# Decode step of two layers: the second attention's scores one unit further ahead on TensorE

## The chip, the cores and the metric

The kernel runs on one core of a Trainium2 chip. The metric is the device time in microseconds (us) of one execution. Engines: TensorE (PE; PEld is its weight load), VectorE (DVE), ScalarE (ACT), GpSimd (POOL) and SyncE (SP), which issues nearly all DMAs.

## The reference, cut to what matters

One token for each of 4 batches passes through attention, a gated layer, the same attention and the same gated layer, each on a layer norm and added to x. The weights and the caches are the same for both layers.

```python
W = 2048                                   # the last 2048 of 8192 cached positions
q = (layernorm(x) @ wq)                    # 32 heads of 128, 8 KV heads, 4 query heads to each
s = einsum("bhqd,bhkd->bhqk", q, k) * 128 ** -0.5
o = einsum("bhqk,bhkd->bhqd", softmax(s), v)
x = x + o @ wo
h = sigmoid(layernorm(x) @ w_gate) * (layernorm(x) @ w_up)   # 512 -> 1792
x = x + h @ w_down                          # then both once more
```

## The kernel before, in words

**Memory.** One SBUF arena holds all that is loaded: 16 buffers of 1 MB for K (two for each KV head) and 9 more that rotate. K is loaded once and stays, transposed in place in the first attention, until the second has used it. V is loaded for each attention; of the last head, one half stays in its buffer and the other is stashed in PSUM and brought back. The output projection wo stays too. `loads` is the list of what is still to come, in a fixed order. Whenever a buffer is released (`done`, or `pool.release` in `score`, line 1078), `fill` takes the next load and writes its DMA into SP's program; it waits there for the last reader of the buffer. For the second attention the list is: V of seven units (14 loads, 1 MB each), w_gate (2), w_up (2) and w_down (3 pieces) of the second gated layer.

**Order.** The kernel is a list of operations. `_Plan.op` works out each one's dependencies from the tokens it reads and writes and from PSUM banks: an operation on a bank waits for all that another engine last did in that bank. From the second attention on `P.chain` is set (line 1296), so TensorE runs its operations exactly in the order in which they are written down, by hand, in `attn_second`. SP too follows that order. VectorE, ScalarE and GpSimd are ordered by `_schedule`, a list scheduler that works with modelled times. Every operation waits for its dependencies in its engine's queue, in order.

**A unit** of the second attention is one KV head with its 16 rows of queries; eight units, 2.0 to 2.7, run from head 7 down to head 0. Its steps:

- `q_unit` (called `qx`): four matmuls spread the unit's queries in bank CB (L721), ScalarE copies them to one of two halves of `qbd` (L726).
- `score`: the mask (L751, 4 matmuls) and the scores (L762, 16) into a bank; it then frees the unit's two K buffers and fills them with the next loads. Unit 2.0 has the bank OBS[0], 2.1 the bank WB, later ones SB[0] and SB[1] in turn.
- `soft`: on VectorE the maximum (L773), its exchange between halves (L777), the mask (L781) and the column's maximum (L785); on ScalarE the exponential (L788) into `prow`, of which there is one only, with the row sums.
- `turn` (`turn_p`): TensorE permutes P (L801), ScalarE copies it back into `prow` (L803), VectorE transposes it into one of two halves of `ebuf` (L808).
- `sum_up`: for units 2.0 to 2.6 `sums`: GpSimd (L904), a matmul (L909), a reciprocal on VectorE (L911), GpSimd (L914). For 2.7 `sums_old`: four small GpSimd steps (L817 to L821), three matmuls (L827), a reciprocal (L834).
- `pv_wide`: 16 matmuls of P times V (L931), transposed (L939), reduced (L944) and moved (L946) on VectorE, added and scaled on GpSimd (L948, L951). For 2.7 it is `pv_unit`, in two halves (L850), with `wo_compact` of unit 2.6 (L1000) between them.
- `back` (`o_back`): two matmuls transpose the result (L965), in bank WB, for unit 2.6 in CB; ScalarE copies it (L971).
- `wo`: the output projection (L984), summed over the units; `wo_back` brings that sum back by a ScalarE copy (L1010) and four matmuls (L1016).

TensorE's order in the loop over u before the change: P times V of u, turn of u+1, back of u-1, scores of u+2, sums of u+1, qx of u+3, projection of u-1. In the last round (u = 6) back and projection of 2.5 come first, then P times V of 2.6, turn of 2.7, `wo_back` and the sums of 2.7.

After the attention come `attn_add` (L1137, L1141), the layer norm and the second `glu`: gate and up matmuls (L1179), transposes (L1188), the product hT (L1206), w_down in three pieces (L1220), copies (L1231) and the output's DMA.

Of the kernel before, what the change touches and what calls it, by code (L numbers as in the profile page):

```python
# [278 lines left out]
def build(nc, A_x, A_k, A_v, A_wq, A_wo, B_wg, B_wu, B_wd, out, cfg=None):  # L279
# [8 lines left out]
    NW = cfg.get("NW", 7)  # L288
# [33 lines left out]
    with es:  # L322
# [559 lines left out]
        def wide_buffers(s, op):  # L882
            f = tile_ap(s).bitcast(F32)
            n = 0
            for name, size in (("tv", 512), ("o32", 32), ("osh", 32), ("rm", 64), ("rv", 8), ("pr", 8)):
                for k2 in range(2):
                    rest[name, k2] = f[:, n:n + size]
                    if name == "tv":
                        rest["dg", k2] = f[:, n:n + 544]
                    n += size  # L890
            for k2 in range(2):
                rest["A", k2] = f[:, n:n + 128].bitcast(BF16)
                n += 128
            rest["op"] = op
            rest["mb"] = f[:, n:n + 64]
            P.op("gpsimd", "mb", 200.0,
                 lambda g: g.tensor_copy(rest["mb"].rearrange("p (b x) -> p b x", b=2),
                                         maskb.unsqueeze(2).broadcast_to([128, 2, 32])),
                 r=[("maskb",)], w=[("mb",)], after=(op,))

        def sums(tag, k2):
            pr, rv, rm = (rest[n, k2] for n in ("pr", "rv", "rm"))
            P.op("gpsimd", "pr" + tag, 200.0,
                 lambda g: g.tensor_scalar(pr, sel_r[:, :], psm[:, k2:k2 + 1], None, ALU.mult),  # L904
                 r=[("psm", k2), ("sel_r",)], w=[("pr", k2)], after=(rest["op"],))
            sbank, c0 = (CB, 256) if tag == "2.0" else (WB, k2 * 8)
            out_ = ps[0:64, sbank, c0:c0 + 8]
            P.op("tensor", "sb" + tag, tm["pe_f32"],
                 lambda pe: pe.matmul(out_, rest["mb"], pr, start=True, stop=True),  # L909
                 r=[("pr", k2), ("mb",)], w=[("psb", k2)], banks=(sbank,))  # L910
            P.op("vector", "ri" + tag, c_dve(8) + 60.0, lambda v: v.reciprocal(rv[0:64, :], out_),  # L911
                 r=[("psb", k2)], w=[("rinv", k2)], banks=(sbank,))
            P.op("gpsimd", "rm" + tag, 250.0,
                 lambda v: v.tensor_tensor(rm[0:64, :].rearrange("p (x e) -> p x e", e=8),  # L914
                                           rv[0:64, :].unsqueeze(2).broadcast_to([64, 8, 8]),
                                           maske[0:64, :].unsqueeze(1).broadcast_to([64, 8, 8]), ALU.mult),
                 r=[("rinv", k2), ("maske",)], w=[("rm", k2)])

        def pv_wide(tag, h, k2, tiles):
            ob = OBS[k2]  # L920
            ew = ebuf[:, k2 * 256:(k2 + 1) * 256].bitcast(BF16).rearrange("p (g n x t) -> p g n t x", g=4, n=2, t=2)
            ss = dict((bp, need(name)) for bp, name in tiles)

            def e_pv(pe):
                last = None
                for n in range(4):
                    mq, t = n // 2, n % 2
                    for g in range(4):
                        jh, bp = g // 2, g % 2
                        src = tile_ap(ss[bp])[:, (jh * 16 + 8 * mq) * 128:(jh * 16 + 8 * mq + 8) * 128]  # L930
                        last = pe.matmul(ps[32 * g:32 * g + 32, ob, :], ew[:, g, mq, t],  # L931
                                         src.rearrange("p (m t d) -> p t m d", t=2, d=128)[:, t], start=(n == 0), stop=(n == 3))
                return last
            P.op("tensor", "PV" + tag, 16 * tm["pe_row"], e_pv,
                 r=tok(ss[0]) + tok(ss[1]) + [("e", k2)], w=[("pso", k2, 0), ("pso", k2, 1)], banks=(ob,))
            for bp, name in tiles:
                done(name)
            tv, o32, osh, rm, av = (rest[n, k2] for n in ("tv", "o32", "osh", "rm", "A"))
            P.op("vector", "tv" + tag, c_dve(512), lambda v: v.transpose(tv, ps[:, ob, :]),  # L939
                 r=[("pso", k2, 0), ("pso", k2, 1)], w=[("tv", k2)], banks=(ob,), after=(rest["op"],))  # L940

            def e_rd(v):
                dg = rest["dg", k2].rearrange("p (m y) -> p m y", m=4)[:, :, 0:128].rearrange("p m (q z) -> p q z m", z=32)[:, :, 0:8, :]
                return v.tensor_reduce(o32.rearrange("p (q x) -> p q x", x=8), dg, AXX, ALU.add)  # L944
            P.op("vector", "rd" + tag, c_dve(128), e_rd, r=[("tv", k2)], w=[("o32", k2)])
            P.op("vector", "sh" + tag, tm["dve_small"], lambda v: v.tensor_copy(osh[0:64, :], o32[64:128, :]),  # L946
                 r=[("o32", k2)], w=[("osh", k2)])
            P.op("gpsimd", "ad" + tag, 250.0, lambda v: v.tensor_tensor(o32[0:64, :], o32[0:64, :], osh[0:64, :], ALU.add),  # L948
                 r=[("o32", k2), ("osh", k2)], w=[("o32", k2)])
            P.op("gpsimd", "av" + tag, 500.0,  # L950
                 lambda v: v.tensor_tensor(  # L951
                     av[0:64, :].rearrange("p (x q e) -> p x q e", x=8, q=4),
                     o32[0:64, :].rearrange("p (q x) -> p x q", x=8).unsqueeze(3).broadcast_to([64, 8, 4, 8]),
                     rm[0:64, :].rearrange("p (x e) -> p x e", e=8).unsqueeze(2).broadcast_to([64, 8, 4, 8]), ALU.mult),
                 r=[("o32", k2), ("rm", k2)], w=[("av", k2)])
            late["tr", tag] = lambda: o_back(tag, k2, av)
# [101 lines left out]
        def attn_second():  # L1058
            hs = list(range(HKV))[::-1]

            def tag(u):
                return "2.%d" % u

            def turn(u):
                turn_p(2, tag(u), u % 2, PBS[0], u < NW)

            def qx(u):
                if u < HKV:
                    q_unit(tag(u), hs[u], u % 2)

            def score(u):
                if u >= HKV:
                    return
                softmax_unit(tag(u), hs[u], True, False)
                if u == 0:
                    soft(0)
                for bp in range(2):
                    pool.release(4 * hs[u] + 2 * bp)
                fill()

            def soft(u):
                if u < HKV:
                    late.pop(tag(u))()

            def sum_up(u):
                if u < NW:
                    sums(tag(u), u % 2)
                elif u < HKV:
                    sums_old(tag(u), u % 2)

            qx(0)
            score(0)
            qx(1)
            q_mms(1, 0, OBS[1], (0, 1))
            score(1)
            turn(0)
            qx(2)
            s = need(wq_part(1, NC - 1, 0)[0])
            left[wq_part(1, NC - 1, 0)[0]] += 1
            q_mms(1, 0, OBS[1], (2, 3))  # L1100
            wide_buffers(s, P.ops[-1])
            sum_up(0)
            q_turn(1, 0, OBS[1], rest["tv", 1], [("tv", 1)], [o for o in P.ops if o.name == "pt2.0"])
            soft(1)
            op = {}

            def wo(u):
                wo_wide(tag(u), hs[u], op[u], u % 2, u == 0, u == NW - 2)

            def back(u):  # L1110
                op[u] = late.pop(("tr", tag(u)))()

            for u in range(NW):
                if u == NW - 1:
                    back(u - 1)
                    wo(u - 1)
                pv_wide(tag(u), hs[u], u % 2, v_tiles[(2, hs[u])])
                turn(u + 1)
                if 0 < u < NW - 1:
                    back(u - 1)  # L1120
                score(u + 2)
                soft(u + 2)
                if u == NW - 1:
                    wo_back()
                sum_up(u + 1)
                qx(u + 3)
                if 0 < u < NW - 1:
                    wo(u - 1)
            u = NW

            def between():
                wo_compact(tag(u - 1), hs[u - 1], late.pop(("tr", tag(u - 1)))(), (u - 1) % 2)
            wo_unit(tag(u), hs[u], pv_unit(tag(u), hs[u], u % 2, v_tiles[(2, hs[u])], between), u % 2, False, True)
# [236 lines left out]
```

## Time and profile before

| what | us |
|---|---|
| median of 6 runs | 184.06 (183.44 to 184.86) |
| the profiled execution's own time | 183.44 |
| its span in the profile | 181.7 |
| TensorE busy, share of the span | 99.5, 55% |
| VectorE busy | 101.7, 56% |
| ScalarE busy | 32.9, 18% |
| GpSimd busy | 21.5, 12% |
| DMA: 72.09 MB | mean 397 GB/s |

The profile is of one execution; its times count from the span's start. The span is less than the execution's own time by 1.7 us, which lie around it. A line of the timeline has start, duration, engine, source line, operation, output and inputs with shape, and how often; in brackets stands the idle time of the engine before it and what ended it. The chain of waits is followed back from the last instruction, at each step to what released it. TensorE's mean granted clock is 0.965 of the full one.

### The profile page before, as it was taken

How to read it: one execution, taken by the hardware profiler on the slowest of the kernel's cores; microseconds unless marked ns; L12 is line 12 of the kernel's file. 1: busy time of each engine (PE TensorE's matmuls, PEld its weight loads, DVE VectorE, ACT ScalarE, POOL GpSimd, SP SyncE). 2: the span in 40 equal slices, each digit the busy share in tenths (PEclk: the TensorE clock that was granted, in tenths of full speed). 3: DMA queues.
4: the chain of work that ended last, by engine and by line, in shares of the span. 5: the costliest groups of instructions: out<-in, count | busy, mean ns of one | idle time of the engine just before them, and what ended most of it. 6: DMA issues, size and time to landing. Idle time of an engine off the chain costs nothing.

```text
span 181.7 us, 3839 instructions
## 1 busy us (share of the span) xinstructions
PE 99.5 (55%) x1627; PEld 53.5 (29%) x1639; DVE 101.7 (56%) x253; ACT 32.9 (18%) x87; POOL 21.5 (12%) x86
## 2 busy tenths in 40 slices
PE   1435325672725619245266566455948876756672
PEld 1002111342411505214136441331213333325531
DVE  6208997758484393653944633122776777744351
ACT  2002032121120301203003001001223444332011
POOL 7000010110010100101001000000012333333000
PEclk9999999999999999999999999999996999999567
DMA  5999999999999999999999999999999999999960
GB/s 190 418 429 433 418 418 415 415 429 415 414 423 418 426 418 416 417 422 426 408 420 418 409 404 409 405 385 390 412 427 420 422 418 424 418 405 407 411 273 20
DMA packets 12305, 72.09 MB, mean 397 GB/s; under 512 B 1144, under 2 KB 1152, under 8 KB 5632
## 3 DMA queue, kind: packets, MB, share of 16 engines
q1 hardware_dynamic: 12280, 71.84, 96.5%
q8 instruction: 13, 0.21, 0.5%
q14 instruction: 4, 0.03, 0.0%
q10 hardware_dynamic: 8, 0.00, 0.0%
HBM read 71.83 MB, written 0.00 MB: 395 GB/s over the span
## 4 chain that ended last, share of the span: by engine, by line
DMA 42%; DVE 24%; PE 22%; SPq 4%; ACT 3%; issue 3%; POOL 0%; DVEq 0%; ACTq 0%
DMA arena<-in_A_v_cache_dram 23%; PE ps L762 9%; DMA arena<-in_B_w_down_dram 9%; DVE arena L733 9%; DMA arena<-in_A_wq_dram 5%; DMA arena<-in_B_w_up_dram 5%; DVE nmax L773 4%; SPq L398 4%; PE ps L751 3%; ACT prow L788 3%; DVE nmax L777 2%; PE ps L850 2%; DVE mxt L781 2%; PE ps L1030 1%; PE ps L674 1%
## 5 line engine op out<-in xcount | busy, mean ns | idle before, releaser
L733 DVE STREAM_TRANSPOSE arena<-arena 128x1024 f32<-128x1024 f32 x32 | 37.0, 1202 | 0.0
L762 PE MATMUL ps<-arena,qbd 128*32 128x512 bf16 x256 | 26.1, 544 | 0.0
L850 PE MATMUL ps<-ebuf,arena 128*128 128x8 bf16 x576 | 17.7, 168 | 9.4 <-DMA arena<-in_A_v_cache_dram 5.3
L773 DVE TENSOR_REDUCE nmax<-ps 128x1 f32<-128x512 f32 x16 | 11.1, 691 | 20.8 <-PE ps L762 20.8
L751 PE MATMUL ps<-msk_m,msk_s 128*32 128x512 bf16 x64 | 8.6, 527 | 22.0 <-DVE arena L733 21.8
L850 PEld LDWEIGHTS ps<-ebuf,arena 128*128 128x128 bf16 x576 | 16.7, 104 | 11.5 <-DMA arena<-in_A_v_cache_dram 6.4
L788 ACT ACTIVATE prow<-ps,nmax 128x512 bf16<-128x512 f32 x16 | 11.0, 687 | 37.9 <-DVE nmax L785 35.5
L726 ACT CAST qbd<-ps 128x256 bf16<-128x256 f32 x16 | 6.0, 373 | 47.9 <-PE ps L762 34.8
L674 PE MATMUL ps<-arena,xn 128*4 128x512 bf16 x64 | 7.9, 577 | 7.6 <-DMA arena<-in_A_wq_dram 6.5
L817 POOL CAST s<-psm 128x1 bf16<-128x1 f32 x9 | 1.7, 188 | 84.6 <-ACT prow L788 84.2
L762 PEld LDWEIGHTS ps<-arena,qbd 128*32 128x32 bf16 x256 | 8.5, 121 | 10.5 <-issue 7.8
L803 ACT CAST prow<-ps 128x512 bf16<-128x512 f32 x16 | 9.4, 586 | 10.9 <-PE ps L801 2.1
L808 DVE STREAM_TRANSPOSE ebuf<-prow 128x256 f32<-128x256 f32 x16 | 7.0, 438 | 5.0 <-ACT prow L803 4.9
L687 DVE STREAM_TRANSPOSE ebuf<-ps 128x512 f32<-128x512 f32 x3 | 2.1, 717 | 11.9 <-PE ps L674 11.8
L751 PEld LDWEIGHTS ps<-msk_m,msk_s 128*32 128x32 bf16 x64 | 1.8, 101 | 23.4 <-DVE arena L733 19.0
L655 ACT ACTIVATE lnv<-ps 128x4 f32<-128x4 f32 x4 | 0.7, 174 | 41.7 <-PE ps L651 41.7
L931 PE MATMUL ps<-arena,ebuf 128*32 128x512 bf16 x112 | 8.1, 415 | 0.0
L721 PE MATMUL ps<-qh,eyew 32*128 32x64 bf16 x64 | 5.7, 220 | 4.3 <-ACT qbd L726 2.4
L1179 PE MATMUL ps<-arena,xn 128*4 128x448 bf16 x64 | 6.6, 553 | 2.4 <-DMA arena<-in_B_w_up_dram 1.6
L858 DVE TENSOR_TENSOR onb<-ps,rinv 128x16 bf16<-128x16 f32 x9 | 1.7, 185 | 10.6 <-PE ps L850 10.6
L801 PEld LDWEIGHTS ps<-prow,perm 128*128 128x128 bf16 x16 | 1.6, 100 | 18.3 <-ACT prow L788 17.9
L939 DVE STREAM_TRANSPOSE arena<-ps 128x512 f32<-128x512 f32 x7 | 5.0, 711 | 3.0 <-PE ps L931 3.0
(105 smaller groups left out, 125.9 us busy)
## 6 DMA issues: line engine op xcount, KB each, us to landing
arena<-in_A_v_cache_dram SPq DMA_DIRECT2D x30, 1024.0 KB, 18.5
arena<-in_A_k_cache_dram SPq DMA_DIRECT2D x16, 1024.0 KB, 25.1
arena<-in_A_wq_dram SPq DMA_DIRECT2D x8, 1024.0 KB, 9.0
arena<-in_A_wo_dram SPq DMA_DIRECT2D x4, 1024.0 KB, 25.0
arena<-in_B_w_gate_dram SPq DMA_DIRECT2D x4, 896.0 KB, 16.2
arena<-in_B_w_up_dram SPq DMA_DIRECT2D x4, 896.0 KB, 15.9
arena<-in_B_w_down_dram SPq DMA_DIRECT2D x2, 1024.0 KB, 12.9
arena<-in_B_w_down_dram SPq DMA_DIRECT2D x1, 768.0 KB, 7.4
```

The source lines that it names most:

```text
L398: o = P.op("sync", name, 0.0, lambda e, dst=dst, src=src: e.dma_start(dst, src), r=r, w=w, dma_bytes=nbytes, dma_rate=tm[rate])
L674: last = pe.matmul(ps[32 * hh:32 * hh + NB, qb, :], xn[:, c * NB:(c + 1) * NB], tile_ap(s)[:, o + hh * 512:o + (hh + 1) * 512], start=(c = ...
L733: P.op("vector", "T%d_%d" % (h, t), c_dve(1024), lambda v, v32=v32: v.transpose(v32, v32), r=[("slot", 4 * h + t)], w=[("slot", 4 * h + t)])
L751: last = pe.matmul(ps[32 * gi:32 * gi + 32, bank, :], msk_s[:, :], msk_m[:, :].unsqueeze(1).broadcast_to([128, 256, 2]), start=True, stop= ...
L762: last = pe.matmul(ps[32 * gi:32 * gi + 32, bank, :], qbd[:, q0:q0 + 32], kt[:, cp // 2, cp % 2, jh * NJ:(jh + 1) * NJ, :], start=False, s ...
L773: lambda v: v.tensor_reduce(nmax[:, k2:k2 + 1], ps[:, bank, :], AXX, ALU.max),
L788: lambda a: a.activation(prow[:, :].rearrange("p (m x t) -> p m x t", x=32, t=2), ps[:, bank, :].rearrange("p (m t x) -> p m x t", x=32, t ...
L803: P.op("scalar", "pc" + tag, c_act(512), lambda a: a.copy(prow[:, :], ps[:, pb, :]), r=[("ppb", pb)], w=[("prow",)], banks=(pb,))
L808: P.op("vector", "pt" + tag, c_dve(256), lambda v: v.transpose(et, prow[:, :].bitcast(F32)), r=[("prow",)], w=[("e", k2)])
L850: last = pe.matmul(ps[:, ob, bp * 8:bp * 8 + 8], src[:, j * 128:(j + 1) * 128], ev[:, j % 2, j % 16 // 2, x0:x0 + 8], start=(j == 0), stop ...
L931: last = pe.matmul(ps[32 * g:32 * g + 32, ob, :], ew[:, g, mq, t], src.rearrange("p (m t d) -> p t m d", t=2, d=128)[:, t], start=(n == 0) ...
L1179: last = pe.matmul(ps[32 * g:32 * g + NB, OBS[n], 0:NF], xn[:, c * NB:(c + 1) * NB], tile_ap(s)[:, o:o + NF], start=(c == 0), stop=(c == N ...
```

## The change

Three things change, and no computation is added or left out.

1. The scores of unit 2.2 are put ahead of the sums of 2.0, and the qx of 2.3 ahead of the loop; in the loop the scores are those of u+3 in place of u+2, and qx that of u+4 in place of u+3. `soft` keeps its place: that of u+2 now comes a round after its scores. The K buffers are freed, and the loads that take them are issued, with the scores.
2. In the last round, the turn of 2.7 and its sums come ahead of P times V of 2.6.
3. The sums of unit 2.6 are in bank CB, no longer in WB.

```diff
-            sbank, c0 = (CB, 256) if tag == "2.0" else (WB, k2 * 8)
+            sbank, c0 = (CB, 256) if tag in ("2.0", "2.%d" % (NW - 1)) else (WB, k2 * 8)
...
             wide_buffers(s, P.ops[-1])
+            score(2)
             sum_up(0)
             q_turn(1, 0, OBS[1], rest["tv", 1], [("tv", 1)], [o for o in P.ops if o.name == "pt2.0"])
             soft(1)
+            qx(3)
...
             for u in range(NW):
                 if u == NW - 1:
                     back(u - 1)
+                    turn(u + 1)
                     wo(u - 1)
+                    sum_up(u + 1)
                 pv_wide(tag(u), hs[u], u % 2, v_tiles[(2, hs[u])])
-                turn(u + 1)
+                if u < NW - 1:
+                    turn(u + 1)
                 if 0 < u < NW - 1:
                     back(u - 1)
-                score(u + 2)
+                score(u + 3)
                 soft(u + 2)
                 if u == NW - 1:
                     wo_back()
-                sum_up(u + 1)
-                qx(u + 3)
+                else:
+                    sum_up(u + 1)
+                qx(u + 4)
                 if 0 < u < NW - 1:
                     wo(u - 1)
```

## The prediction

> **What bounds the kernel now.** I read the page's slices first, then the chain that ended last, the SP queue, the tail instruction by instruction, and the DMA rate by stretch. The slices:
>
> ```profile
> DMA  5999999999999999999999999999999999999960
> GB/s 190 418 429 433 418 418 415 415 429 415 414 423 418 426 418 416 417 422 426 408 420 418 409 404 409 405 385 390 412 427 420 422 418 424 418 405 407 411 273 20
> ```
>
> The 16 DMA engines are full from 4.5 us to about 174 us. 71.8 MB have to come in, and no slice of the second attention (about 126 to 169 us) has a hole. The chain shows the attention first, one unit every 4.29 us, and then leaves it for a DMA:
>
> ```profile
> 151.93 0.70 DVE nmax L773
> ...
> 153.55 0.79 ACT prow L788 x2
> ...
> 154.38 0.39 PE ps L801
> ...
> 155.23 0.94 PE ps L762 x14
> 156.19 0.70 DVE nmax L773
> ...
> 162.52 0.38 SPq L398
> ...
> 162.94 15.76 DMA arena<-in_B_w_down_dram
> ...
> 178.74 0.31 PE ps L1220 x8
> ```
>
> Within a unit, scores (L762), maximum (L773), exponential (L788), permutation (L801) and the next scores form one ring: 156.19 - 151.93 = 4.26. But the last 16 us are one transfer, the last piece of w_down, which waits in line behind the others. SP shows that the line is long:
>
> ```profile
> 144.96 3.40 SPq L398 DMA_DIRECT2D arena<-in_B_w_gate_dram  x2
> 148.40 8.84 SPq L398 DMA_DIRECT2D arena<-in_B_w_up_dram  x2
> 157.29 6.69 SPq L398 DMA_DIRECT2D arena<-in_B_w_down_dram  x3
> ```
>
> An issue takes 0.37 us when there is room (w_gate's first). These take about 4.4 us each: SP is held back by a full queue, not by a buffer. From the trace's semaphore records (16 increments per transfer, one for each engine's share) I take when transfers are complete: V of unit 1 at 134.0, of unit 5 at 155.1, of unit 6 at 160.0, of unit 7 at 162.5 and 165.0, second half of w_up at 174.4, the w_down pieces at 176.8, 178.1 and 178.7. The first increments come every 2.48 us per MB without a gap. The last increment trails the first by 1.6 us at 126 us and by 3.7 us at the end: a few engines are late.
>
> The tail:
>
> ```profile
> 176.87 0.22 DVE L1206 TENSOR_TENSOR hT<-ebuf,qbd 128x56 bf16<-128x56 f32 x1
> 177.20 0.46 PEld L1220 LDWEIGHTS ps<-arena,hT 128*4 128x4 bf16 x32 [1.31 <-DMA arena<-in_B_w_down_dram]
> 177.23 0.62 PE L1220 MATMUL ps<-arena,hT 128*4 128x128 bf16 x32 [1.04 <-DVE hT L1206]
> 178.12 0.21 PEld L1220 LDWEIGHTS ps<-arena,hT 128*4 128x4 bf16 x16 [0.46 <-DMA arena<-in_B_w_down_dram]
> 178.12 0.40 PE L1220 MATMUL ps<-arena,hT 128*4 128x128 bf16 x16 [0.27 <-DMA arena<-in_B_w_down_dram]
> 178.74 0.28 PE L1220 MATMUL ps<-arena,hT 128*4 128x128 bf16 x8 [0.23 <-DMA arena<-in_B_w_down_dram]
> ```
>
> Two paths meet here. Compute: hT at 177.09, after which the three groups would take 0.62 + 0.40 + 0.28 = 1.30, from 177.23 to 178.53. DMA: the third piece at 178.70, the last group done at 179.02. So compute has 179.02 - 178.53 = **0.5 us of slack**, and the DMA sets the end. After it come fixed copies and the output, up to 181.7. The last view is the DMA by stretch:
>
> ```profile
> 174.00:175.00 1.00, 1.00 (x14) 0.72 (x14) 0.65 (x1) 0.37 (x3) 0.00 (x0) 0.50 0.84 336
> 175.00:176.00 1.00, 1.00 (x24) 0.37 (x12) 0.61 (x3) 0.35 (x3) 0.00 (x0) 0.68 0.51 207
> 176.00:177.00 1.00, 0.18 (x8) 0.00 (x0) 0.96 (x3) 0.00 (x0) 0.00 (x0) 1.00 0.26 107
> 177.00:178.00 1.00, 0.62 (x32) 0.46 (x32) 0.08 (x1) 0.00 (x0) 0.00 (x0) 1.00 0.23 88
> ```
>
> The last three numbers are granted clock, DMA share and GB/s. From 176 on, a quarter of the engines is still working: the stragglers finish alone.
>
> **What the Trainium skill says.** "DMA: Bandwidth & Descriptors", section "Why a DMA increments its semaphore by 16 and not by 1": the engines of one transfer finish independently, and only the full count means that all landed. The trace agrees (3.7 us between first and last increment). "Runtime: NRT & Kernel Launch", section "Instruction fetch mechanics": an engine's instructions come in 16 KiB blocks over a DMA queue of its own. The page's third part has q8 with 13 packets and 0.21 MB, so 16 KB each, and the straggling grows by 1.0 us where one of them ran at 136.8. The change adds no instruction, so I expect the same 13. "TensorE: Matmul & The Clock Gate", section "What's actually happening": the clock is halved after idle windows. Here it was 0.5 from 138.1 to 141.5 and from 168.8 to 175.6; at half clock the 16 P x V matmuls took 1.90 us against 1.04.
>
> **The change, part by part.**
>
> *Scores one unit further ahead.* S(2) is moved ahead of the first unit's P x V, and inside the loop S(u+3) takes the place of S(u+2), as qx(u+4) does of qx(u+3). No work is added: per unit still 0.40 mask, 1.1 scores, 0.28 qx on TensorE. What goes is the ring. The maximum of u+2 then finds its scores done a unit earlier. Left over is the ring of the one buffer prow: exponential 0.88, permutation 0.39, copy 0.59, transpose 0.45, with steps of about 0.06 between, 2.5 us. VectorE has 0.69 + 0.33 + 0.25 + 0.21 + 0.16 + 0.72 + 0.38 + 0.18 + 0.45 = 3.37 a unit, with gaps of 0.03 about 3.6; TensorE about 3.4 (154.38 to 157.76). So a unit can fall from 4.29 to about 3.6, 0.7 x 6 = 4 us in all, **but V arrives at one unit per 5 us**. The second half of unit 7's P x V, now at 168.25, can't start before 165.0. The attention gains at most **3.2 us**.
>
> *What the loads do.* S(u) frees two K buffers, so each V and weight load can be issued about one unit (4.29 us) earlier; order and sizes stay. SP's queue is full from 145 on and no engine runs dry before that: earlier issues only wait longer in line. Worth **0**. Its cover is the full queue; were it gone, an issue would be earlier, never later.
>
> *Start-up.* S(2), 0.40 + 1.47 at the first units' rate, now stands ahead of unit 0's sums, and qx(3), 0.28, ahead of its P x V. qx(3) writes the bank in which unit 0's sums lie, so it waits for their reciprocal on VectorE, which may stand behind unit 1's maximum (done at 136.2). P x V(0), now at 133.5, may start at up to 136.6, 3.1 late. Its transpose was taken up at 136.09 anyway, and the permutation of unit 1, at 137.03, waits for its exponential. After a P x V up to 137.65 that is **0 to 0.6 us** late; I take 0.6.
>
> *Sums of the seventh unit in bank CB.* The transposition of unit 5 (162.31) waited for the reciprocal of unit 6 (162.01) because both use bank WB. That wait goes: part of the gain above, at most the 1.3 us that TensorE idled there.
>
> *Last P turned ahead of its V.* Permutation (0.39) and sums of unit 7 (0.22) move ahead of P x V(6). The sums wait for four GpSimd steps of 0.19 with gaps, 163.02 to 164.00: a new wait of 1.0 us after the last exponential, with P x V(6), the output projection and unit 6's whole back end queued behind it. On GpSimd these four stand ahead of unit 6's steps, as they do now. Its gain is that transpose and P of unit 7 are ready at once. Taken together with the order now, from the last exponential to the last half P x V: before 168.25 - 162.96 = 5.3; after 1.35 + 1.04 + 2.3 (VectorE and GpSimd to unit 6's transposition, by 164.34 to 166.80 now) + 1.0 = 5.7, **0 to 0.4 us worse**, covered because the last exponential itself no longer waits for S(7) and can be up to 2 us earlier (unit 6's transpose was done at 160.14, the exponential started at 162.18).
>
> *Sum.* Attention ends 3.2 us earlier at best, and 0.6 + 0.4 = 1.0 later if nothing of the ring is gained; likeliest 1.5 to 3 earlier. Then w_up is late next: hT at the earliest 174.4 + 0.74 (half of the 16 matmuls of 1.48) + 0.59 + 0.22 + 0.1 = 176.0, against 177.09. And then the DMA: last piece 178.70, unchanged. **Change of the span: 0.**
>
> The sum is against the profiled execution, 183.44 us (span 181.7, 1.7 around it), the fastest of six. The median is 0.62 higher. Whether that is DMA or a run in which compute was late by more than its 0.5 us the page can't say; the second kind would be cured. I take a quarter of it: 184.06 - 0.16 = **183.9**.
>
> **The rivals.**
>
> *A: the DMA still sets the end* (forecast): 183.4 to 184.4. For it: full queue, gapless increments, 0.5 us of slack. Against it: nothing in the page, only that the six runs spread by 1.4 us.
>
> *B: faster, the stragglers are fewer.* If the instruction blocks or other traffic fall on other engines, the remaining work of 0.84 + 0.51 + 0.26 + 0.23 + 0.08 = 1.9 us after 174 ends at 175.9; compute then ends at 176.0 + 0.14 + 1.30 = 177.4 instead of 179.02: 1.6 less, 182.5. It needs compute to be earlier too, which this change gives. Against it: nothing in the change moves bytes between engines.
>
> *C: slower, P x V waits for work that isn't its own.* P x V(0) starts 3.1 us late behind qx(3), and VectorE's planned order puts each maximum behind the transpose before it, so that the ring stays at 0.88 + 0.39 + 0.59 + 0.45 + 1.5 + steps = 4.2 and the loss is carried to the end. It decides from 0.5 (slack) + 0.9 = 1.4 us carried; at 2.0 carried, with the tail's 0.4 added, 184.06 + 1.9 = 186.0; at 1.5, 185.1. For it: the planner's order is by modelled times. Against it: VectorE has 0.9 us to spare per unit, and V's pace is slower than the ring.
>
> *D: the order doesn't come out as stated*, since engines other than TensorE are ordered by the planner: same time as A, 184.06.
>
> **How the numbers follow.** A 0.63, D 0.07, B 0.18, C 0.12. About 0.5% (0.9 us) is what a measurement of this kernel can tell from no change. A and D lie within it but for 0.02 on the faster side: faster 0.2, same 0.68, slower 0.12. The range has to leave out at most 0.2: from the upper part of B (182.9) to the lower part of C (185.1).
>
> **What would show it.** Right: last w_down piece at 178.7 within 0.5; the chain ends in the same transfer; units of about 5 us with P x V waiting for V's DMA; PE idle before w_up at 174. Ring broken: no wait of the permutation for the exponential of 0.9 us. Wrong: a last landing before 178 (B), or hT later than 177.6 with the chain running through attention (C).

## The result, and the profile after

The changed kernel takes 183.6 us (median of 36 runs, 182.77 to 184.07), the kernel before 184.13 (73 runs, 183.07 to 186.12). The ratio is 0.9965 with a 95% interval of 0.9952 to 0.9978: 0.64 us less, 0.4 to 0.9. The lowest times differ by 0.3 us, the highest by 2.05: what the change takes away is mostly the upper part of the old spread.

The profiled execution of the changed kernel took 183.27 us, its span 181.5. The slices of its page are as full as before:

```profile
DMA  5999999999999999999999999999999999999960
GB/s 199 415 428 431 421 418 418 412 428 417 415 422 419 422 419 415 417 424 426 408 422 415 409 404 413 406 385 382 421 417 424 424 419 421 419 410 410 408 280 20
```

In the second attention, TensorE's timeline shows P x V of units 2.0, 2.1, 2.2 and 2.3 (start, duration):

```profile
134.69 1.05 PE L931 MATMUL ps<-arena,ebuf 128*32 128x512 bf16 x16
138.45 1.05 PE L931 MATMUL ps<-arena,ebuf 128*32 128x512 bf16 x16 [0.18 <-DVE nmax L785]
...
141.85 1.05 PE L931 MATMUL ps<-arena,ebuf 128*32 128x512 bf16 x16
145.20 1.04 PE L931 MATMUL ps<-arena,ebuf 128*32 128x512 bf16 x16
```

Unit 2.2 takes 3.35 us (145.20 - 141.85) where a unit took 4.29. From unit 2.4 on V is late instead. P x V of 2.5 and 2.6 and the two halves of 2.7 wait for it, and a unit takes 5.36 us (160.28 - 154.92):

```profile
154.92 1.05 PE L931 MATMUL ps<-arena,ebuf 128*32 128x512 bf16 x16 [1.67 <-DMA arena<-in_A_v_cache_dram]
...
160.28 1.05 PE L931 MATMUL ps<-arena,ebuf 128*32 128x512 bf16 x16 [0.29 <-DMA arena<-in_A_v_cache_dram]
...
162.69 0.96 PE L850 MATMUL ps<-ebuf,arena 128*128 128x8 bf16 x32 [0.38 <-DMA arena<-in_A_v_cache_dram]
...
165.20 1.01 PE L850 MATMUL ps<-ebuf,arena 128*128 128x8 bf16 x32 [0.31 <-DMA arena<-in_A_v_cache_dram]
```

The last half P x V starts at 165.20 (before: 168.25). Then the tail:

```profile
174.18 0.92 PE L1185 MATMUL ps<-arena,xn 128*4 128x448 bf16 x8 [1.34 <-DMA arena<-in_B_w_up_dram]
...
175.84 0.22 DVE L1212 TENSOR_TENSOR hT<-ebuf,qbd 128x56 bf16<-128x56 f32 x1
...
176.63 1.02 PE L1226 MATMUL ps<-arena,hT 128*4 128x128 bf16 x32 [1.11 <-DMA arena<-in_B_w_down_dram]
...
177.85 1.02 PE L1226 MATMUL ps<-arena,hT 128*4 128x128 bf16 x24 [0.20 <-DMA arena<-in_B_w_down_dram]
```

hT is ready at 176.06, 1.03 us earlier than before. It can't be earlier, because the last matmuls ahead of it wait for the second half of w_up, and behind it TensorE waits for w_down. The chain of waits no longer runs through the units' ring:

```profile
160.28 1.07 PE ps L931 x16
161.35 0.65 SPq L398
...
162.05 15.77 DMA arena<-in_B_w_down_dram
177.81 0.04 issue
177.85 0.60 PE ps L1226 x16
```

By the semaphore records the pieces of w_down are complete at 176.6, 177.8 and 178.45 (before 176.8, 178.1 and 178.70). Three us earlier at the attention's end are 1 us at hT and 0.2 us at the end of this execution. So the question is where the 0.64 us over all the runs come from.

### The profile page after: what moved, and what is told of

It reads as the page before. It is cut to its first block, busy times and chain, and to the rows that moved or that the text cites. A ratio compares the mean times of both kernels' runs of the same rounds, so it can differ in the third digit from the quotient of the medians.

```text
span 181.5 us, 3837 instructions
## 1 busy us (share of the span) xinstructions
PE 100.3 (55%) x1627; PEld 53.7 (30%) x1639; DVE 101.2 (56%) x253; ACT 32.5 (18%) x87; POOL 21.3 (12%) x86
## 4 chain that ended last, share of the span: by engine, by line
DMA 54%; DVE 20%; PE 15%; SPq 4%; issue 3%; ACT 3%; DVEq 0%; ACTq 0%
DMA arena<-in_A_v_cache_dram 35%; DMA arena<-in_B_w_down_dram 9%; DVE arena L733 9%; PE ps L762 6%; DMA arena<-in_A_wq_dram 5%; DMA arena<-in_B_w_up_dram 5%; SPq L398 4%; DVE nmax L773 3%; PE ps L751 2%; ACT prow L788 2%; PE ps L850 2%; PE ps L1030 1%; DVE ps L507 1%; DVE arena L517 1%; DVE nmax L777 1%
## 5 line engine op out<-in xcount | busy, mean ns | idle before, releaser
L762 PE MATMUL ps<-arena,qbd 128*32 128x512 bf16 x256 | 25.4, 531 | 0.0
L931 PE MATMUL ps<-arena,ebuf 128*32 128x512 bf16 x112 | 7.3, 381 | 3.4 <-DMA arena<-in_A_v_cache_dram 2.0
L1030 PE MATMUL ps<-onp,arena 128*128 128x16 bf16 x144 | 5.3, 175 | 2.4 <-DVE onp L873 2.4
```

Source lines behind the costliest of these rows:

```text
L762: last = pe.matmul(ps[32 * gi:32 * gi + 32, bank, :], qbd[:, q0:q0 + 32], kt[:, cp // 2, cp % 2, jh * NJ:(jh + 1) * NJ, :], start=False, s ...
L1030: last = pe.matmul(ps[:, WB, c * NR:(c + 1) * NR], tile_ap(s)[:, o + r_ * D + c * 128:o + r_ * D + (c + 1) * 128], ov[:, r_ * NR:(r_ + 1) ...
```

## The experiments

The theories that the expectations name: (1) in most executions of the kernel before, compute was late, and the change takes it out of the DMA's way; (2) the gain is made in the last rounds; (3) the DMA alone sets both ends, and the order has no part in it. In the diffs below, a sign shows the edit against the kernel that the text names. Ratios are to the kernel before.

**The scores ahead alone**: the kernel before with

```diff
+            score(2)
             sum_up(0)
...
+            qx(3)
...
-                score(u + 2)
+                score(u + 3)
...
-                qx(u + 3)
+                qx(u + 4)
```

> The change's first part alone (scores and qx one unit further ahead), its tail as before. Theory 1, compute is brought out of the way of the DMA by the broken ring: all of the gain is here, ratio to the kernel before 0.995 to 0.998, units paced by V at about 5 us, last piece of w_down at 178.5 within 0.4, chain ending in it. Theory 2, the gain is the last rounds' doing (bank CB, last P ahead of its V): ratio 0.999 to 1.002 and the last half P x V near 168. Theory 3, the DMA's stragglers moved by chance and TensorE's order has no part: the last landing and the time move together, whatever the order.

Measured: 0.9967 (0.9954 to 0.9980), the chain ends in w_down (complete at 179.1, later than the 178.9 that I had allowed). Within the intervals the whole gain is here. The last landing of this execution was 0.4 us later than the first profile of the kernel before had it, and the median of the runs is still lower than that of the kernel before: as far as one trace tells, the gain is not an earlier landing.

**The last rounds alone**: the kernel before with the bank CB for the sums of 2.6, and turn and sums of 2.7 ahead of P x V of 2.6 (the rest of the change's diff).

> The change's second and third part alone (last P and its sums ahead of P x V of 2.6, sums of 2.6 in bank CB), scores two units ahead as before. Theory 1: the ring of 4.29 us a unit stands, the last half P x V starts between 167.5 and 168.6, ratio 0.998 to 1.003. Theory 2: ratio 0.995 to 0.998 and the last half P x V before 167. Theory 3: ratio anywhere within 0.003 of 1, following the last landing alone.

Measured: 1.0029 (1.0008 to 1.0049), slower by 0.5 us. In the timeline of its profiled execution the last permutation waits, with P x V of 2.6 behind it:

```profile
162.79 0.69 ACT L788 ACTIVATE prow<-ps,nmax 128x512 bf16<-128x512 f32 x1 [0.79 <-DVE nmax L785]
...
163.62 0.61 PE L801 MATMUL ps<-prow,perm 128*128 128x512 bf16 x1 [1.83 <-ACT prow L788]
```

1.83 us of TensorE go by waiting for that exponential, and the last half P x V starts at 170.18, later than I had allowed (168.6); P x V of 2.6 fell into half clock in this execution, which is 0.86 us of it. Theory 2 falls. Its part of the change is a cost by itself. With the scores ahead, so that the exponential is early, it does no harm that shows: 0.9965 with it, 0.9967 without.

**A delay of 1.44 us behind the attention, in both kernels**:

```diff
+            for n in range(2 if L == 2 else 0):
+                P.op("vector", "dly%d" % n, c_dve(512), lambda v: v.transpose(ebuf[:, :], ps[:, OBS[0], :]),
+                     r=[("psw",)], w=[("dly",), ("e", 0), ("e", 1)], banks=(OBS[0],))
...
-                 r=[("psw",)], w=[("x2",)], banks=(WB,))
+                 r=[("psw",), ("dly",)], w=[("x2",)], banks=(WB,))
```

> The kernel before with two idle transposes of 0.72 us on VectorE, 1.44 us, between the second attention's end and the layer norm. Theory 1: the profiled execution had 0.5 us of slack and typical ones less, so 0.9 to 1.4 us come through, ratio 1.005 to 1.008. Theory 3, in which compute is well ahead in all executions and the DMA alone decides: ratio 1.000 to 1.002.

> The changed kernel with the same 1.44 us. Theory 1: its compute has 1.7 us before the second half of w_up would be late and 0.6 us behind that, so nothing comes through: ratio 0.995 to 0.998 to the kernel before, as without the delay. If instead the gain is compute time that still sets the end in the changed kernel, 1.4 us come through and the ratio is 1.003 to 1.005.

Measured: the kernel before 1.0096 (1.0059 to 1.0133), so 1.8 us later (1.1 to 2.5), a little more than expected; the changed kernel 0.9971 (0.9955 to 0.9987), the same as without the delay. The kernel before with the delay ends in compute:

```profile
178.82 0.23 DVE hT L1209
...
179.18 1.69 PE ps L1223 x56
```

The last piece of w_down was complete at 178.87 in this execution. I estimate from this trace that without the 1.49 us of transposes the 56 matmuls would have ended at 179.4 (180.87 - 1.49), and that the DMA alone would have allowed 179.3 (178.87, and 0.45 for the last eight matmuls at half clock). So a typical execution of the kernel before has no slack, and the delay comes through whole. The changed kernel has at least 1.4 us.

**Twice that delay in the changed kernel** (4 transposes, 2.88 us):

> The changed kernel with 2.88 us of idle transposes on VectorE between the second attention and the layer norm. Theory 1 with 2.3 us in hand: 0.3 to 1.0 us come through, ratio to the kernel before 0.998 to 1.002. With more than 3 us in hand: 0.996 to 0.998, as without a delay.

Measured: 0.9974 (0.9956 to 0.9992); medians 183.8 and 183.7 with 2.88 and 1.44 us of delay. Of its profiled execution, 184.21 us, the chain ends in compute again, hT being ready at 177.99 and the last piece at 178.87; by the same estimate compute is 0.5 us late there, so that about 2.4 us were in hand. By the medians hardly any of the 2.88 us comes through. The change leaves 2.4 to 2.8 us in hand, at least the 2.3 that I had counted; the interval doesn't tell it from the second reading.

**One transfer less in both kernels**:

```diff
-                for cc in range(NC // 2):
+                for cc in range(1 if (nm, k) == ("wg", 1) else NC // 2):
...
-                    name = (nm, c // 2, k)
+                    name = (nm, 0 if (nm, k) == ("wg", 1) else c // 2, k)
```

> The kernel before with one transfer less: the second half of the second gated layer's w_gate (0.875 MB, 2.2 us of DMA) isn't loaded, its matmuls read the first half twice. Theory 1, compute sets the end in most executions of the kernel before: the shorter DMA brings 0 to 0.5 us, ratio 0.997 to 1.000. Theory 3, the DMA alone sets the end in both kernels: 2.2 us less down to the compute path's own end, so ratio 0.988 to 0.994.

> The changed kernel with the same transfer left out. Theory 1: here the DMA sets the end and compute has 2 us in hand, so all of the 2.2 us come through: ratio to the kernel before 0.983 to 0.987. If compute still sets the end of the changed kernel: ratio 0.994 to 0.997.

Measured: the kernel before 0.9991 (0.9964 to 1.0018), the changed kernel 0.9825 (0.9785 to 0.9864): nothing (0.7 us at most) against 3.2 us (2.5 to 4.0), of which 0.64 is the change's own. With the same 2.2 us of DMA taken away, one kernel doesn't move beyond the noise and the other moves by all of it. The chains of the two say it in a line each. The kernel before without the transfer:

```profile
177.66 0.23 DVE hT L1206
...
178.02 1.40 PE ps L1220 x55
```

The changed kernel without it:

```profile
159.97 16.89 DMA arena<-in_B_w_down_dram
...
176.90 0.33 PE ps L1226 x8
```

This settles between theories 1 and 3: in a typical execution compute set the end before, and the DMA does after.

**The kernel before once more, for its profile**:

> The kernel before, unchanged, for a second profile. Theory 1: if this execution takes 184 us or more, its w_down pieces have landed before hT is ready, the three groups of matmuls run without a wait between them, and the chain ends in compute; if it takes 183.5 or less it looks as the first profile did. Theory 3: the chain ends in the last w_down piece whatever the time.

Measured: 184.83 us, and in the main what theory 1 says: the chain ends in compute and the matmuls run without a wait between them. Only the last piece of w_down landed behind hT and not ahead of it. The rows of the stretches 159.9 to 163.3, 163.3 to 166.7 and 166.7 to 170.1 (the seventh entry is the granted clock), then three lines of its timeline:

```profile
159.90:163.30 3.40, 1.74 (x28) 0.65 (x20) 1.97 (x7) 0.99 (x4) 1.04 (x3) 1.00 1.00 407
163.30:166.70 3.40, 3.16 (x25) 1.54 (x25) 0.77 (x2) 1.05 (x5) 0.76 (x4) 0.50 1.02 406
166.70:170.10 3.40, 2.60 (x73) 2.42 (x74) 1.09 (x4) 0.49 (x2) 1.15 (x3) 1.00 1.03 406
```

```profile
163.92 1.92 PE L931 MATMUL ps<-arena,ebuf 128*32 128x512 bf16 x16
...
178.40 0.22 DVE L1206 TENSOR_TENSOR hT<-ebuf,qbd 128x56 bf16<-128x56 f32 x1
...
178.76 1.66 PE L1220 MATMUL ps<-arena,hT 128*4 128x128 bf16 x56 [0.67 <-DVE hT L1206]
```

In this execution TensorE's clock is halved from 163.3 to 166.7, just where P x V of 2.6 stands: 1.92 us in place of the 1.04 of the first profile, whose first spell lay at 138.1. hT comes at 178.62, the matmuls start on it and not on the DMA (last piece 178.98), and run at half clock again, 1.66 us for the 56. The execution is 1.4 us longer than the first profiled one.

The times of the other runs fit this. Of the 136 runs of the kernel before that ran beside these experiments, the 62 with a mean granted clock of 0.96 or more have a median of 183.9 us, the 74 with a lower one 184.6. Among the changed kernel's runs the clock makes no such difference (183.6 us both below 0.94 and above). So the kernel before is late where its clock is low, and the changed kernel isn't. That is a relation over many runs; which spell made each of them late is not shown.

**Filling TensorE's wait ahead of that place**: the kernel before with

```diff
+            def busy(n):
+                def e_busy(pe):
+                    last = None
+                    for _ in range(n):
+                        for gi in range(4):
+                            last = pe.matmul(ps[32 * gi:32 * gi + 32, SB[0], :], msk_s[:, :],
+                                             msk_m[:, :].unsqueeze(1).broadcast_to([128, 256, 2]), start=True, stop=True)
+                    return last
+                P.op("tensor", "busy", n * tm["pe_sq"], e_busy, r=[("msk_s",), ("msk_m",)], w=[("pss", 0)], banks=(SB[0],))
...
                 if u == NW - 1:
+                    busy(6)
                     back(u - 1)
```

> The kernel before with 24 idle mask matmuls (1.3 us) put where TensorE waits for the reciprocal of unit 2.6, ahead of the transposition of 2.5 in the last round. They write a bank that nobody reads again. If the executions with late compute come from a half-clock spell that this wait brings on, right where the last P x V stands, the spell goes: P x V of 2.6 takes 1.04 us and not 1.9, ratio to the kernel before 0.996 to 0.998, as the change has. If the clock has no part in it, or other idle times bring the spell on as well: ratio 0.999 to 1.003.

Measured: 0.9983 (0.9958 to 1.0008), 14 runs from 183.26 to 184.43. Inconclusive: half of the gain in the middle of the interval, no change within it. In its profile P x V of 2.6 takes 1.03 us, but so it did in the first profile without the filling. There is a hint for it: all 14 runs have a mean clock of 0.95 or more, while 11 of the 35 runs of the kernel before beside them lie below 0.95. That the spells at this place make the kernel before late is shown for one execution; that the wait brings them on is not.

**What sets the DMA's end.** Two runs on the changed kernel, whose end is the DMA's. First, fewer matmuls in the first layer:

```diff
-                for cp in range(4):
+                for cp in (0, 3) if tag[0] == "0" else range(4):
...
-                    for j in range(2 * NJ):
+                    for j in (0,) if tag[0] == "0" else range(2 * NJ):
...
-                for r_ in range(REP):
+                for r_ in (0, REP - 1) if tag[0] == "0" else range(REP):
...
-                    for fc in range(a, b):
+                    for fc in sorted({a, b - 1}):
```

> The changed kernel with most matmuls of the first layer left out (one of 32 in each half P x V, two of four groups in scores and output projection, 4 of 14 in w_down), some 1,300 TensorE instructions less, 5 blocks of 256, with all transfers of data, waits and the second layer as they are. If the 16 KB instruction blocks on queue 8 make the late DMA engines late (the spread between first and last increment grew by 1.2 and 1.0 us beside two of 13), then with 8 or 9 blocks hardly an engine has two: spread at the end 2.3 to 2.9 us instead of 3.6, last landing and end 0.7 to 1.2 us earlier, ratio 0.990 to 0.993. If the blocks have no part in it: spread 3.6, ratio 0.995 to 0.998.

Measured: 0.9862 (0.9812 to 0.9912), twice what I expected. In its profile, with eight blocks, seven of them within the span,

```profile
q8 instruction: 7, 0.11, 0.3%
```

the last piece is complete at 176.36, 2.1 us earlier than in the changed kernel. The spread between first and last increment is 2.2 us in place of 3.5, and the first increment itself comes 0.7 earlier. So this kernel's end follows the DMA one for one: its span is 2.0 us shorter. Second, more matmuls:

```diff
+                for _ in range(80 if tag[0] == "0" else 0):
+                    last = pe.matmul(ps[:, CB, 256:264], perm[:, :], perm[:, 0:8], start=True, stop=True)
```

> The changed kernel with 80 idle matmuls (128x8) ahead of the qx of each unit of the first attention, 1280 TensorE instructions more, 5 blocks of 256, all work and all transfers of data kept. If the instruction blocks on queue 8 delay the DMA stream, as the run with fewer matmuls suggests with 2.1 us for 5 blocks, then 18 blocks: spread over 4.2 us at the end, last landing and end 0.8 to 2.1 us later, ratio to the kernel before 1.001 to 1.008. If that run was faster for its lighter first layer: 13 blocks or 18 make no difference, spread 3.6, ratio 0.995 to 0.998.

Measured: 1.0267 (1.0216 to 1.0319), far more than either reading, and the spread at its end is 2.5 us, with 18 blocks, where I had expected over 4.2. The slices of its page show why its time tells nothing on the blocks:

```profile
GB/s 196 424 424 426 417 411 420 419 416 424 409 423 417 426 421 403 428 421 421 408 422 217 224 331 382 421 350 416 427 423 416 423 417 419 416 417 408 409 343 13
```

From 98 to 107 us the DMA engines moved only about half of what they did elsewhere, and less than elsewhere up to 112. I put this down to the added 2.13 us a unit, which held up the first attention, so that it freed its buffers late; no run tests that.

Its trace does tell something on the blocks, by when they ran. The first one ran at 30.8 us in the kernel before, and the spread went from 0.4 to 1.6 us with the transfer complete at 34.4. With more matmuls it ran at 19.4, and the spread went from 0.4 to 1.8 with the transfer complete at 22.0. Later blocks at 79.7 and 152.8 took it from 1.9 to 3.3 (at 83.2) and from 1.8 to 2.6 (at 155.5); between them, in the stretch with little to move, it fell to 1.0. So the jumps of the spread move with blocks, though most blocks bring none, and the number of blocks alone doesn't set the spread at the end. How much of the 2.1 us in the run with fewer matmuls is due to the blocks, and how much to the lighter first layer, stays open.

**A smaller last piece**: the changed kernel with

```diff
-            return bounds if k < NG else bounds[:-1] + [(bounds[-1][0], NFC - 2), (NFC - 2, NFC)]
+            return bounds if k < NG else bounds[:-1] + [(bounds[-1][0], NFC - 2), (NFC - 2, NFC - 1), (NFC - 1, NFC)]
```

> The changed kernel with the last piece of w_down, 256 KB, loaded as two of 128 KB, each with its own four matmuls. The DMA sets the end, and the matmuls behind the last landing become 4 in place of 8: 0.1 to 0.2 us less, ratio to the kernel before 0.9950 to 0.9965. If the smaller rows or one more transfer cost as much as that: 0.9965 to 0.998.

Measured: 0.9967 (0.9949 to 0.9985), as the changed kernel: no gain to be seen, but one of 0.1 us would not show in this interval.

## Why the prediction was right, and where its sum was off

*The DMA sets the end* (rival A): right for the changed kernel. The last piece came at 178.45 against the 178.70 written down, the chain ends in it, and the one-transfer run shows it directly. That it does so still, as it did before, holds for the profiled execution only; in a typical one compute set the end. The time came out in the range because what this was worth is small.

*The ring breaks, V becomes the limit*: right. A unit takes 3.35 us (I had 3.6) until V is late and about 5 after that, and the last half P x V starts at 165.20 (I had 165.0 at best). hT at 176.06 was put at 176.0.

*The start-up costs 0 to 0.6 us*: wrong in sign. P x V of 2.0 starts at 134.69, 1.2 later, but the exponential of 2.1 starts at 135.35 where it started at 136.20. With the sums of 2.0 later, VectorE took the transpose of q and unit 2.1's maximum first (the maximum at 133.64 in place of 134.59) and no longer stood 0.64 us waiting for the sums. The reciprocal was done at 134.4 and held qx(3) by 0.6 us, not by 3.

*The last P ahead of its V costs up to 0.4 us, covered by an earlier exponential*: the sign right, the size a little low. The term of 2.3 in it should be 2.46 (166.80 - 164.34), which makes the sum 5.85 and the cost 0.55. Alone it costs 0.5 us (0.15 to 0.9), and 5.3 us between the last exponential and the last half P x V became 6.6 (163.57 to 170.18), not 5.7; 0.86 of the difference is P x V of 2.6 at half clock, 1.90 in place of 1.04. In the changed kernel it is covered.

*Earlier loads are worth nothing*: right as far as it shows. By the trace the first w_gate load is issued at 141.24 in place of 144.96, the second one's issue then takes 6.50 us instead of 2.99, so that it ends at 148.2 where it ended at 148.4, and the first increments come at the same 2.48 us per MB.

*The slack of 0.5 us, and a quarter of 0.62 us*: this is the term that was mis-sized. The gain is 0.64 us (0.4 to 0.9), four times the 0.16 that I took. I read the slack from one execution, the fastest of six, in which the three w_down groups ran at full clock (1.30 us). At half clock they take 1.66, and another spell at P x V of 2.6 costs 0.88: then compute is late by about 0.75 us (1.66 + 0.88 - 1.30 - 0.49). The delay run gives the typical slack: none, within its interval. I had named this case, compute late in some of the runs, and left it at a quarter because the page couldn't decide it; the other five times, all 0.2 to 1.4 us above the profiled one, were evidence for it that I gave too little weight.

Two smaller slips changed nothing. In rival C, 1.5 us carried with the tail's 0.4 added give 185.5 by the same sum, not 185.1. And of the issues said to take about 4.4 us each, three do (4.3 to 4.7); the second of w_gate takes 2.99, and the last two of w_down 0.9 and 1.0.

## What to carry to other kernels

Where two paths meet at the end within half a microsecond, one profile doesn't tell which of them is the bound: read how far the runs spread, and settle it by a delay on one path and a cut on the other, in both kernels. A change that takes compute out of the DMA's way gains only as much as compute was late, however much earlier the stage ends, here 0.64 us out of 3. And a step moved ahead of its need, as the last P was, costs time unless what it waits for has become earlier as well.

## What the runs showed of the hardware that I had not expected

TensorE's half-clock spells fall at different places in executions of the same program: 138.1 to 141.5 and 168.8 to 175.6 in one, 163.3 to 166.7 and from 170.1 on in the other. In each of the eight traces in which the clock changes more than once, the changes lie a whole number of 3.41 us apart.

The prediction had the clock halved after idle windows. How long TensorE was busy just before doesn't explain a spell alone. In the first profile it was busy for 1.07 of the 3.4 us ahead of 138.1 and for 2.16 ahead of 168.8. In the second it was busy for 1.74 from 159.9 to 163.3, where the spell followed, and for 1.55 from 136.0 to 139.4, where the clock stayed full.

The changed kernel ran at half clock from 164.6 us to its end, and it cost about 0.1 us: the last matmuls behind the last landing took 0.41 us in place of 0.31, and what stood before them waited for the DMA anyway.

A transfer's late engines don't catch up while the stream is full: in the kernel before the spread between first and last increment never fell by more than 0.2 us from 0.4 at 6 us to 3.7 at the end. It fell from 3.2 to 1.0 us in the run in which the stream thinned out.
